# Sparse attention and a gated MLP on one Trainium2 core: the rows of q and k of heads 6 and 7 are loaded first, on both queues, and the first lines of the first batch's list of steps are set anew

## The chip, the cores and the metric

The kernel runs on one core of a Trainium2 chip as a single program. The metric is device time in microseconds (us) of one execution. The core has five engines that run their own instruction streams and meet at semaphores: PE (matmuls and transposes), DVE (vector work), ACT (activations, copies and, here, also DMA issues), POOL (vector work, memsets) and SP (DMA issues alone). DMAs are issued from two queues in this kernel, SP's and ACT's.

## What is computed

Attention over 8 batches and 8 heads of 576 tokens with 64 features each; heads 0 to 3 see a local window of 32 tokens, heads 4 to 7 see every 32nd token. Its output, heads side by side, is the input x of a gated MLP with a spatial gate (a 576 x 576 matrix over the tokens). Everything is float32.

```python
scores = np.matmul(q, k.transpose(0, 1, 3, 2)) / np.sqrt(D)
mask_local   = (rel >= 0) & (rel < 32)
mask_strided = (rel >= 0) & (pos[None, :] % 32 == pos[:, None] % 32)
scores = np.where(mask, scores, -1e9)          # heads 0-3 local, 4-7 strided
attn = np.exp(scores - scores.max(-1, keepdims=True))
attn = attn / (attn.sum(-1, keepdims=True) + 1e-9)
x = np.matmul(attn, v)                          # (8, 576, 512)
h = gelu_tanh(x @ w_in)
u, v = h[..., :512], h[..., 512:]
v_n = layernorm(v) * g_ln
v_s = np.einsum('ts,bsd->btd', w_sg, v_n) + b_sg[None, :, None]
out = x + (u * v_s) @ w_out
```

## The kernel before

The kernel treats the 8 batches one after the other. All its work is cut into some 80 kinds of steps, each a small function, and three hand-written lists set the order in which the steps are written out: `START` for the first batch (with everything that has to be loaded or converted once), `CYCLE` for the middle batches and `LAST` for the last one. A word of a list names a step, and after a colon which piece. `=` marks work that belongs to no batch, `-` work of this batch, no sign work for the next batch, `+` work for the one after it. A `^` sends those parts of a step that can go to either of two engines to the second one (loads from SP to ACT, some vector work between DVE and POOL). Each engine executes its instructions in the order in which the lists emit them, with no reordering by a scheduler, and the DMAs of both queues are numbered in the order of the lists too. Eight DMA semaphores are handed out in turn to that numbered sequence, so the ninth DMA waits, on the queue that issues it, until the first has landed, and so on: at most eight are under way, and a queue that waits for a slot holds back everything behind it.

The steps that matter here:

- **Rows of q and k** (`LP`, function `qk_rows`, line 449). For a pair of heads `hh` (0 and 1 are local, 2 and 3 strided; pair 3 is heads 6 and 7) four DMAs of 144 KB bring in two heads of q and two of k, by 96 partitions in pieces of 256 bytes. `TP` (`qk_turn`) transposes one of the two tiles on PE in six pieces; its argument is 2 x pair, plus 1 for k, so `TP:6` is q of pair 3 and `TP:7` its k. `TC` (`qk_turned`) copies the result from PSUM to `qT` or `kT` on ACT. The row tiles share four buffers.
- **Scores and softmax of pair 3**: `SS:3` (64 matmul instructions in the trace, tile `ss`), `MK:3` adds the mask on DVE (two instructions, tile `sms`), `MX:3` the maximum and `SB^:3` the subtraction on DVE, `EX:3` the exponential on ACT. `SL:0` and `SL:1` are the scores of the local pairs (tile `sa`), `MK:4` the mask of their first part (tile `sml`, `sm_mask`), on DVE.
- **Conversion of the weights.** `w_in` and `w_out` come as 64-bit floats and are turned into two float32 parts with integer operations. `w_in` has eight pieces of 512 KB (`cl:0` to `cl:7`, tile `stage`), `w_out` eight of 256 KB (`cl:8` and on, tile `cs`). A piece goes through `ca` (exponent field, DVE), `cb` (ACT), `cc` (two instructions, DVE), `cd` (ACT), `ce` (low word, DVE; with `^` on ACT and then POOL), `cf` (value, POOL; with `^` DVE), `cg` (high part, ACT) and `ch` (low part, POOL; with `^` DVE).
- **Later in the first batch**: `LP:2` loads the rows of pair 2, issued from ACT; `wb` and `wc` clear and load the bias row `bst`; `wl:1` loads a block of the token matrix (`wsg`). The matmuls of the MLP proper begin with `v` (tiles `v`, from `va:0` on).

Every instruction that goes through the recording helper shows line 83, so groups are told apart by their tiles.

Of the kernel before, what the change touches and what calls it, by code (L numbers as in the profile page):

```python
# [21 lines left out]


START = """
mk= mp= cl=:3 ca=:3 cl=:1 LP-^:3 cb=:3 cc=:3 ca=:1 cb=:1 cl=:0 cc=:1 cd=:1 cd=:3 cl=:2 TZ-:0
ca=:2 cl=:8 ml= ce=:3 ca=:0 cb=:0 ce=^:1 TP-^:6 TC-:6 cb=:2 TP-^:7 TC-:7 cf=^:1 cg=:1 cc=:2
cd=:2 LP-:0 SS-:3 LP-:1 TZ-:1 ca=:8 cb=:8 ch=:1 cc=:0 cd=:0 cl=:9 ce=^:0 TP-:1 MK-:3 TP-:0 TC-:0
MX-:3 SB-^:3 TC-:1 ce=:2 EX-:3 cf=^:2 LP-^:2 TP-^:2 TC-:2 SL-^:0 MK-:4 ca=:9 TP-^:3 TC-:3 SL-:1
MX-:4 wb= SB-:4 cl=:6 ca=:6 cb=:6 cc=:6 cl=^:4 cc=:8 LZ-:0 wc= wd= we= LZ-:1 wl=:1 MK-:5 MX-:5
cf=^:3 EX-:4 TP-:4 TC-:4 SU-:4 SB-:5 LP:1 SU-:3 cg=:2 ch=:2 cd=:8 TP-:5 cf=:0 wt=:1 TC-:5 SS-^:2  # L30
cd=:6 cg=:3 cl=^:7 EX-:5 mr= ML-:4 SU-:5 TP^:2 TC:2 MK-:2 MX-:2 cg=:0 ch=:0 TZ:0 ce=^:6 LV-:0
ML-^:5 ca=:4 TP:3 TZ:1 TC:3 wh=:1 ch=:3 wm=:1 ca=:7 SB-^:2 PL-:4 CL-:4 PL-^:5 CL-:5 CM-:5 VX-:0
VY-:0 XR-:0 EX-:2 SU-:2 cb=:4 cc=:4 ML-^:2 LP:0 TP^:0 cb=:7 LV-:1 TC:0 XHa-:0 XLa-:0 ce=^:8
cf=:8 TP^:1 TC:1 cb=:9 cc=:9 XHb-:0 XLb-:0 cf=^:6 cl=:5 PS-^:2 CS-:2 ca=:5 XD-:0 SL^:0 SL:1 MK:0
VA-:1 XH-:1 XL-:1 cd=:4 cc=:7 LV-:2 PV-^:2 PW-:2 XH-:2 cd=:9 ce=:9 wo= wp= ML-:3 LP:2 XR-:1 MX:0
PS-:3 CS-:3 cb=:5 SB:0 XD-:1 va:0 vb:0 cl=^:13 TP^:4 TC:4 XL-:2 vc:0 LV-:3 PV-:3 XR-:2 PW-:3
cd=:7 XH-:3 cc=:5 TP^:5 EX:0 ce=:4 cf=^:4 cg=:4 ch=:4 va:1 XL-:3 xt LP:3 vd:0 g:0 XD-:2 vb:1
ce=:7 XR-:3 cf=^:9 ls:0 lr^:0 wl=:0 TP^:6 TC:6 cd=:5 cl=^:15 vc:1 cf=:7 cg=:7 cg=:9 vd:1 TP:7
# [3 lines left out]
ca=:15 ca=:10 cb=:10 cb=:15 u:0 SU:0 wh=:4 cc=:10 wl=:3 wm=:4 cc=:15 cd=:10 ce=:10 cf=:10 MK:2  # L42
wt=:2 LQ+:0 ug:0 wh=:2 wm=:2 cl=^:11 wt=^:3 wh=:3 wm=:3 ML:0 lh:2 ll:2 cg=:13 u:3 ll:1 cd=:15
ca=:11 ce=^:15 cb=:11 cc=:11 PL:0 CL:0 ch=:13 ug:3 MX:3 SB^:3 s:3 cd=:11 ce=:11 cf=:11 cg=:11
CM:0 s^:2 cf=^:15 MX:2 SB^:2 s^:0 ch=^:11 sm:3 sm:2 cl=^:12 ca=:12 TZ+:1 EX:3 SU:3 sh:2 sl:2 s:1
sh:3 cb=:12 ML^:3 LZ:0 cg=:10 cc=:12 VA^:1 cd=:12 LQ+:3 sm:0 ch=:8 cg=:15 cl=:14 ch=^:10 ca=:14
ch=^:15 ce=^:12 cf=:12 sh:0 sl^:0 TQ+:0 cg=:12 LV:0 sm:1 sh:1 sl:1 r cb=:14 cc=:14 EX:2 LQ+:1
VA:0 XR:1 PS:3 CS:3 o:0 o^:1 ch=:12 sl:3 cd=:14 ce=:14 cf=^:14 cg=:14 SU:2 ML^:2 XH:0 XL:0
ch=:14 XH:1 XL:1 LV:3 o^:2 o^:3 o2:2 os:2 XD:1 XR:0 XD:0 o2:0 o2:3 os:3 LV:2 PS^:2 o2:1 PV:3
# [52 lines left out]
def tile_sparse_attention_moe(  # L102
# [14 lines left out]
    pe, dve, act, pool, sp = (  # L117
        InOrder(tc, e) for e in (nc.tensor, nc.vector, nc.scalar, nc.gpsimd, nc.sync)
    )
# [9 lines left out]
    TP = S // NCL  # L129
# [14 lines left out]
    def loads():  # L144

        return act if alt[0] else sp
# [299 lines left out]

        return b < 2

    def qk_rows(b, hh):

        for nm, src in (("q", q), ("k", k)):
            raw = p1.tile([P, RT, 2, D], F32, tag="raw", name=f"row{nm}_{b}_{hh}", bufs=4)
            for hp in range(2):
                loads().dma_start(
                    raw[0:RP, :, hp], src[b, 2 * hh + hp].rearrange("(p c) d -> p c d", c=RT)
                )
            state[b, hh, "row" + nm] = raw
# [506 lines left out]
    def out_send(b, kk):  # L964
# [6 lines left out]

    STEPS = {

        "LQ": qk_load, "LP": qk_rows, "TP": qk_turn, "TC": qk_turned, "TQ": qk_transpose, "LV": v_load, "TZ": k_zeros, "LZ": v_zeros, "SL": local_scores,
        "SS": strided_scores, "MK": sm_mask, "MX": sm_max, "SB": sm_sub, "EX": sm_exp,
        "SU": sm_sum, "ML": sm_mul, "PL": local_pt, "CL": local_pt_copy, "CM": local_pt_last,
        "VA": lambda b, hh: local_pv(b, hh, range(NJ)),
# [81 lines left out]
```

## Time and profile before

| | us |
|---|---|
| median of 3 runs | 581.92 |
| the three runs | 580.87, 581.92, 583.30 |
| span of the profiled execution, first to last instruction | 581.7 |
| PE busy | 550.2 (95% of the span) |
| DVE busy | 398.9 (69%) |
| ACT busy | 270.4 (46%) |
| POOL busy | 190.1 (33%) |

The page gives the span of the profiled execution and nothing around it; the median of the runs lies 0.2 us above that span, and their spread is 2.4 us. PE is busy almost throughout. Its idle time is found in the first tenth of the span, where weights are converted, the first heads are loaded and the first softmaxes run; that is the part that the change touches. To read it, take the views by stretch of time (how busy each engine is from here to there), the chain of waits (what released the work that ended last) and the timeline (each instruction with its start).

### The profile page before, as it was taken

Reading aid. Unit: us, or ns where it says so; the run is one execution under the profiler, and the core shown is the slowest. Engines: PE = TensorE matmul, PEld = TensorE weight load, DVE = VectorE, ACT = ScalarE, POOL = GpSimd, SP = SyncE. Lnnn points to the kernel's source line nnn. Section 1 sums busy time; section 2 is a strip of 40 time slices with the busy share of each in tenths; the row PEclk is TensorE's granted clock in tenths of the full one; section 3 lists DMA queues with packets and bytes.
Section 4 is the critical chain, followed back from the end, with each engine's and each line's share of the span. In section 5 each row is a group of like instructions: output and inputs, shape, how many; then the busy total and the mean of one; then the engine's idle time right before and its main releaser. Section 6 shows DMA issues by size and latency. Waiting matters only on the chain.

```text
span 581.7 us, 14975 instructions
## 1 busy us (share of the span) xinstructions
PE 550.2 (95%) x6129; PEld 493.7 (85%) x6129; DVE 398.9 (69%) x692; ACT 270.4 (46%) x396; POOL 190.1 (33%) x452
## 2 busy tenths in 40 slices
PE   0778999999899999999999999999999999999996
PEld 0667798978898889988998889988998889988995
DVE  4798898877774687567874687567774686545532
ACT  4566766622662248332652258332662247433320
POOL 3363484201722045311722045311722045302310
PEclk9986999999999999999999999999999999999999
DMA  8796665868832894259922894259822870055002
GB/s 233 207 174 161 141 159 92 188 138 151 186 55 61 177 192 72 42 134 176 171 42 65 175 195 67 41 137 177 167 42 61 180 177 1 1 122 155 2 1 90
DMA packets 261478, 69.95 MB, mean 120 GB/s; under 512 B 247137, under 2 KB 247137, under 8 KB 261410
## 3 DMA queue, kind: packets, MB, share of 16 engines
q1 hardware_dynamic: 172386, 46.11, 37.4%
q10 hardware_dynamic: 89024, 22.88, 18.6%
q8 instruction: 48, 0.79, 0.6%
q14 instruction: 20, 0.16, 0.1%
HBM read 50.09 MB, written 18.87 MB: 119 GB/s over the span
## 4 chain that ended last, share of the span: by engine, by line
PE 64%; DVE 11%; POOL 7%; ACT 5%; DMA 5%; issue 5%; ACTq 2%; SPq 0%; DVEq 0%; POOLq 0%
PE sg L83 18%; PE o L83 15%; PE v L83 11%; PE u L83 7%; POOL nt L83 4%; PE os L83 3%; PE ol L83 3%; ACTq L83 2%; POOL y L83 2%; PE pts L83 2%; DMA rowk<-in_k_dram 2%; PE sa L83 2%; DVE sr L83 1%; ACT L83 1%; ACT vg L83 1%
## 5 line engine op out<-in xcount | busy, mean ns | idle before, releaser
L83 PE MATMUL sg<-wsh,vg 128*128 128x288 f32 x512 | 113.2, 296 | 1.0 <-ACT ptl L83 0.8
L83 PE MATMUL u<-xt,wih 128*128 128x288 f32 x512 | 104.1, 298 | 2.6 <-ACT u L83 2.4
L83 PE MATMUL o<-woh,vg 128*128 128x512 f32 x288 | 95.5, 397 | 0.0
L83 PEld LDWEIGHTS sg<-wsh,vg 128*128 128x128 f32 x512 | 85.5, 188 | 2.0 <-ACT ptl L83 1.0
L83 PEld LDWEIGHTS u<-xt,wih 128*128 128x128 f32 x512 | 82.0, 188 | 4.8 <-ACT u L83 3.7
L83 PE MATMUL v<-wih,xt 128*128 128x512 f32 x256 | 83.9, 397 | 0.0
L83 ACT ACT_TABLE_LOAD x40 | 51.3, 1283 | 53.4 <-DMA xd<-xs 33.9
L83 PE MATMUL u<-xt,wil 128*128 128x288 f32 x256 | 75.5, 295 | 0.0
L83 PE MATMUL sg<-wsl,vg 128*128 128x288 f32 x256 | 75.3, 294 | 0.0
L83 PEld LDWEIGHTS o<-woh,vg 128*128 128x128 f32 x288 | 54.1, 188 | 11.1
L83 PEld LDWEIGHTS v<-wih,xt 128*128 128x128 f32 x256 | 48.0, 188 | 11.0
L83 PE MATMUL o<-wol,vg 128*128 128x512 f32 x144 | 56.3, 391 | 0.0
L83 DVE TENSOR_TENSOR ob<-o,xn 128x512 f32<-128x512 f32 x32 | 22.1, 689 | 44.4 <-PE o L83 43.6
L83 ACT CAST vg<-gt 128x576 fp32r<-128x576 f32 (+2 forms) x48 | 22.8, 509 | 61.1 <-DVE gt L83 61.1
L83 PE MATMUL v<-wil,xt 128*128 128x512 f32 x128 | 50.1, 392 | 0.0
L83 PEld LDWEIGHTS sg<-wsl,vg 128*128 128x128 f32 x256 | 48.2, 188 | 0.0
L83 PEld LDWEIGHTS u<-xt,wil 128*128 128x128 f32 x256 | 48.0, 188 | 0.1
L83 DVE TENSOR_TENSOR gt<-sg,u 128x576 f32<-128x576 f32 x32 | 23.6, 739 | 22.1 <-PE sg L83 12.4
L83 DVE BATCH_NORM_STATS2 bnst<-hv 128x6 f32<-128x512 f32 (+1 forms) x40 | 27.1, 676 | 16.8 <-ACT hv L83 16.8
L83 POOL TENSOR_TENSOR sms<-sms,sr 100x576 f32<-100x576 f32 x13 | 15.1, 1160 | 61.1 <-DVE sr L83 61.1
L83 DVE SCALAR_TENSOR_TENSOR vg<-hv,y,vg 128x512 fp32r<-128x512 f32 x32 | 23.0, 761 | 15.7 <-ACT vg L83 15.7
L83 PEld LDWEIGHTS o<-wol,vg 128*128 128x128 f32 x144 | 27.1, 188 | 4.9
(152 smaller groups left out, 1071.1 us busy)
## 6 DMA issues: line engine op xcount, KB each, us to landing
xd<-xs ACTq DMA_DIRECT2D x128, 72.0 KB
v<-in_v_dram SPq DMA_DIRECT2D x62, 144.0 KB
xn<-xd SPq DMA_DIRECT2D x8, 1024.0 KB
out_dram<-ob ACTq DMA_DIRECT2D x32, 256.0 KB
rawq<-in_q_dram SPq DMA_DIRECT2D x96, 72.0 KB
rawk<-in_k_dram SPq DMA_DIRECT2D x96, 72.0 KB
v<-in_v_dram SPq DMA_DIRECT2D x30, 128.0 KB
stage<-in_moe_w_in_dram SPq DMA_DIRECT2D x6, 512.0 KB
```

Source lines behind the costliest of these rows:

```text
L83: ins = self.tc.keep_in_program_order(op(*args, **kwargs))
```

## The change

Three things are edited. `qk_rows` takes a pair of queues and, where it is given one, issues q from the first and k from the second. A new step `LB` calls it with SP for q and ACT for k. And the first four lines of `START` are set anew: `LB-:3` stands at the very front in place of `LP-^:3` (which had all four DMAs on ACT, behind the first two pieces of `w_in` on SP), and the transposes, copies, scores and softmax of pair 3 and the loads of pair 0 and 1 stand earlier among the conversion steps.

```diff
 START = """
-mk= mp= cl=:3 ca=:3 cl=:1 LP-^:3 cb=:3 cc=:3 ca=:1 cb=:1 cl=:0 cc=:1 cd=:1 cd=:3 cl=:2 TZ-:0
-ca=:2 cl=:8 ml= ce=:3 ca=:0 cb=:0 ce=^:1 TP-^:6 TC-:6 cb=:2 TP-^:7 TC-:7 cf=^:1 cg=:1 cc=:2
...
+LB-:3 mk= mp= cl=:3 cl=:1 TZ-:0 TP-^:6 TC-:6 TP-^:7 TC-:7 ca=:3 cb=:3 LP-:0 cl=:0 SS-:3 cc=:3
+ca=:1 cb=:1 ml= cd=:3 MK-:3 MX-:3 cl=:2 SB-^:3 cc=:1 cd=:1 EX-:3 ce=:3 LP-:1 TZ-:1 ca=:0 cb=:0 ce=^:1
...
-    def qk_rows(b, hh):
+    def qk_rows(b, hh, queues=None):
 
-        for nm, src in (("q", q), ("k", k)):
+        for x, (nm, src) in enumerate((("q", q), ("k", k))):
+            queue = queues[x] if queues else loads()
             raw = p1.tile([P, RT, 2, D], F32, tag="raw", name=f"row{nm}_{b}_{hh}", bufs=4)
             for hp in range(2):
-                loads().dma_start(
+                queue.dma_start(
...
+        "LP": qk_rows, "LB": lambda b, hh: qk_rows(b, hh, (sp, act)),
```

What this does to SP's queue, at its beginning, with the semaphores that each issue waits for (DMAHW0 to DMAHW7 are the eight slots; `stage` is a piece of `w_in`, `rowq_3` the q rows of pair 3, `rowq_0` those of pair 0). Before:

```order
L83 DMA stage<-in_moe_w_in_dram 128x1024 x4
L83 DMA cs_147<-in_moe_w_out_dram 128x512 [waits DMAHW0_49]
L83 DMA rowq_0_204<-in_q_dram 96x6x64 [waits DMAHW1_49]
L83 DMA rowq_0_204<-in_q_dram 96x6x64 [waits DMAHW2_49]
L83 DMA rowk_0_207<-in_k_dram 96x6x64 [waits DMAHW3_49]
L83 DMA rowk_0_207<-in_k_dram 96x6x64 [waits DMAHW4_49]
```

and with the change, the same place:

```order
L83 DMA rowq_3_102<-in_q_dram 96x6x64 x2
L83 DMA stage<-in_moe_w_in_dram 128x1024 x2
L83 DMA rowq_0_152<-in_q_dram 96x6x64 x2
L83 DMA rowk_0_155<-in_k_dram 96x6x64 [waits DMAHW0_49]
L83 DMA rowk_0_155<-in_k_dram 96x6x64 [waits DMAHW1_49]
L83 DMA stage<-in_moe_w_in_dram 128x1024 [waits DMAHW2_49]
L83 DMA stage<-in_moe_w_in_dram 128x1024 [waits DMAHW3_49]
```

The q rows of pair 3 now go ahead of all weights, the rows of pair 0 ahead of the third and fourth piece, and these two pieces wait for slots 2 and 3, which the k rows of pair 3 (on ACT's queue) hold.

On ACT, from its first work to the DMAs of pair 2 (`cv` is a conversion buffer, `wih` the high part of `w_in`, `sms` the softmax tile of pair 3). Before:

```order
L83 DMA rowq_3_125<-in_q_dram 96x6x64 x2
L83 DMA rowk_3_128<-in_k_dram 96x6x64 x2
L83 ACTIVATE cv_122<-cv_122,ebias 128x512
L83 ACTIVATE cv_134<-cv_134,ebias 128x512
L83 ACTIVATE stage<-stage 128x512 x2
L83 ACTIVATE cv_175<-cv_175,ebias 128x512
L83 ACTIVATE stage<-stage 128x512
L83 COPY qT_3_187<-turnq_3_180 128x576
L83 ACTIVATE cv_145<-cv_145,ebias 128x512
L83 COPY kT_3_197<-turnk_3_190 128x576
```

and with the change:

```order
L83 DMA rowk_3_105<-in_k_dram 96x6x64 x2
L83 COPY qT_3_138<-turnq_3_131 128x576
L83 COPY kT_3_147<-turnk_3_140 128x576
L83 ACTIVATE cv_149<-cv_149,ebias 128x512
L83 ACTIVATE cv_194<-cv_194,ebias 128x512
L83 ACTIVATE stage<-stage 128x512 x2
L83 ACTIVATE sms_100<-sms_100 100x576
L83 ACTIVATE cv_242<-cv_242,ebias 128x512
L83 ACTIVATE stage<-stage 128x512
L83 COPY qT_0_263<-turnq_0_256 128x576
L83 COPY kT_0_129<-turnk_0_249 128x576
L83 ACTIVATE cv_266<-cv_266,ebias 128x512
```

Both copies of pair 3 now stand ahead of the first conversion step on ACT, and the exponential of pair 3 ahead of the third `cv`; behind these rows come, in both, the rest of the first conversions and then the DMAs of pair 2.

On DVE, from the second conversion on. Before:

```order
L83 SCALAR_TENSOR_TENSOR cv_134<-stage,cv_134 128x512
L83 TENSOR_SCALAR stage<-stage 128x512
L83 TENSOR_SCALAR cv_145<-stage 128x512
L83 SCALAR_TENSOR_TENSOR stage<-stage 128x512
L83 TENSOR_SCALAR cv_175<-stage 128x512
L83 TENSOR_TENSOR cv_134<-stage,cv_134 128x512
L83 SCALAR_TENSOR_TENSOR cv_145<-stage,cv_145 128x512
L83 TENSOR_SCALAR stage<-stage 128x512
L83 TENSOR_SCALAR cx<-cs_147 128x256
L83 SCALAR_TENSOR_TENSOR cv_175<-stage,cv_175 128x512
L83 TENSOR_SCALAR stage<-stage 128x512
L83 TENSOR_TENSOR sms_100<-ss_3_210,mask_s 36x576 x2
```

and with the change, from the same conversion buffer's first operation (`cv_194` is what `cv_134` was):

```order
L83 TENSOR_SCALAR cv_194<-stage 128x512
L83 TENSOR_TENSOR sms_100<-ss_3_159,mask_s 36x576 x2
L83 TENSOR_REDUCE mx_3_225<-sms_100 100x16
L83 TENSOR_TENSOR sms_100<-sms_100,mx_3_225 100x576
L83 SCALAR_TENSOR_TENSOR cv_194<-stage,cv_194 128x512
L83 TENSOR_SCALAR stage<-stage 128x512
L83 SCALAR_TENSOR_TENSOR stage<-stage 128x512
L83 TENSOR_SCALAR cv_242<-stage 128x512
L83 TENSOR_SCALAR cv_266<-stage 128x512
```

Mask, maximum and subtraction of pair 3 stood behind the first operations of all four pieces of `w_in` before; now they stand after those of the first piece and the exponent field of the second, and the rest of the conversions stands behind them. The number of instructions on each engine is the same, and the number of DMAs too; from the fifth line of `START` on the lists agree.

More of the change, by code (lines that the diff above doesn't have):

```diff
@@ L24 @@
 START = """
-mk= mp= cl=:3 ca=:3 cl=:1 LP-^:3 cb=:3 cc=:3 ca=:1 cb=:1 cl=:0 cc=:1 cd=:1 cd=:3 cl=:2 TZ-:0
-ca=:2 cl=:8 ml= ce=:3 ca=:0 cb=:0 ce=^:1 TP-^:6 TC-:6 cb=:2 TP-^:7 TC-:7 cf=^:1 cg=:1 cc=:2
-cd=:2 LP-:0 SS-:3 LP-:1 TZ-:1 ca=:8 cb=:8 ch=:1 cc=:0 cd=:0 cl=:9 ce=^:0 TP-:1 MK-:3 TP-:0 TC-:0
-MX-:3 SB-^:3 TC-:1 ce=:2 EX-:3 cf=^:2 LP-^:2 TP-^:2 TC-:2 SL-^:0 MK-:4 ca=:9 TP-^:3 TC-:3 SL-:1
+LB-:3 mk= mp= cl=:3 cl=:1 TZ-:0 TP-^:6 TC-:6 TP-^:7 TC-:7 ca=:3 cb=:3 LP-:0 cl=:0 SS-:3 cc=:3
+ca=:1 cb=:1 ml= cd=:3 MK-:3 MX-:3 cl=:2 SB-^:3 cc=:1 cd=:1 EX-:3 ce=:3 LP-:1 TZ-:1 ca=:0 cb=:0 ce=^:1
+cl=:8 TP-:1 TP-:0 TC-:0 TC-:1 ca=:2 cb=:2 cc=:0 cd=:0 cf=^:1 cg=:1 cc=:2 cd=:2 ch=:1 ca=:8 cb=:8
+cl=:9 ce=^:0 ce=:2 cf=^:2 LP-^:2 TP-^:2 TC-:2 SL-^:0 MK-:4 ca=:9 TP-^:3 TC-:3 SL-:1
 MX-:4 wb= SB-:4 cl=:6 ca=:6 cb=:6 cc=:6 cl=^:4 cc=:8 LZ-:0 wc= wd= we= LZ-:1 wl=:1 MK-:5 MX-:5
@@ L972, in tile_sparse_attention_moe @@
     STEPS = {
-        "LQ": qk_load, "LP": qk_rows, "TP": qk_turn, "TC": qk_turned, "TQ": qk_transpose, "LV": v_load, "TZ": k_zeros, "LZ": v_zeros, "SL": local_scores,
+        "LQ": qk_load, "LP": qk_rows, "LB": lambda b, hh: qk_rows(b, hh, (sp, act)),
+        "TP": qk_turn, "TC": qk_turned, "TQ": qk_transpose, "LV": v_load, "TZ": k_zeros, "LZ": v_zeros, "SL": local_scores,
         "SS": strided_scores, "MK": sm_mask, "MX": sm_max, "SB": sm_sub, "EX": sm_exp,
```

## The prediction

> **What bounds the kernel now.** I first read how busy each engine is by stretch (columns: from:to, length, busy time and instructions of PE, PE's weight loads, DVE, ACT, POOL, then the clock granted to PE, the DMA share, GB/s), because the change touches the opening alone.
>
> ```profile
> 0.00:5.00 5.00, 0.00 (x0) 0.00 (x0) 1.53 (x7) 1.49 (x2) 3.83 (x23) 1.00 0.49 173
> 5.00:28.00 23.00, 11.74 (x235) 10.38 (x238) 14.43 (x28) 12.80 (x21) 6.09 (x11) 1.00 0.90 227
> 28.00:48.00 20.00, 15.10 (x179) 12.76 (x168) 19.07 (x37) 14.57 (x29) 11.30 (x16) 0.78 0.91 185
> 56.00:576.00 520.00, 514.60 (x5503) 463.01 (x5502) 356.68 (x609) 237.97 (x340) 165.53 (x399) 1.00 0.54 112
> ```
>
> From 56 us on PE is busy 514.6 of 520 us: whatever makes that stretch start earlier or later moves the end by as much. From 28 to 48 DVE is busy 19.07 of 20 us and its order there is unchanged. Only from 5 to 28 us is there slack to win: DVE is busy 14.43 of 23 us. The chain of waits says what filled it:
>
> ```profile
> 3.70 10.45 DMA rowk<-in_k_dram
> 14.15 0.14 issue
> 14.29 1.21 PE turnk L83 x6
> 15.49 0.02 issue
> 15.52 0.65 ACT kT L83
> ...
> 27.39 0.70 DVE cv L83
> ...
> 47.16 1.55 PE pts L83 x8
> ...
> 55.92 2.79 PE v L83 x12
> ```
>
> The k rows of pair 3 (issued from ACT) landed at 14.15 us; from 27.39 on DVE's row of work sets the pace (first step `cc` of w_in piece 6), up to PE's matmuls. So the question is when DVE reaches that step, now 27.39 us. I call its shift **d**; the time is the old one plus d.
>
> **First part: when do the rows of pair 3 land (R)?** Now: 14.15.
>
> ```profile
> 0.79 1.95 SPq L83 DMA_DIRECT2D stage<-in_moe_w_in_dram  x4
> 1.07 1.41 ACTq L83 DMA_DIRECT2D rowq<-in_q_dram  x2
> 2.51 3.02 ACTq L83 DMA_DIRECT2D rowk<-in_k_dram  x2
> 5.24 0.49 DVE L83 TENSOR_SCALAR cv<-stage 128x512 int32<-128x512 int32 x1
> 1.00:2.00 1.00, 0.00 (x0) 0.00 (x0) 0.00 (x0) 1.00 (x1) 0.96 (x4) 1.00 0.04 8
> 4.00:10.00 6.00, 0.00 (x0) 0.00 (x0) 4.16 (x10) 1.46 (x3) 1.48 (x7) 1.00 1.04 343
> 15.00:19.00 4.00, 3.27 (x70) 2.91 (x70) 3.12 (x7) 3.32 (x6) 0.30 (x2) 1.00 0.93 207
> ```
>
> First bytes move at about 2.0 us (8 GB/s in the slice before it). While little but rows travel (15 to 19 us) the rate is 207 GB/s, with weights (4 to 10 us) 343. The four transfers of pair 3 are 4 x 147 KB = 590 KB, 2.85 us at 207. Landing costs a bit more: the first 524 KB piece needs 2.0 + 1.5 = 3.5 us at 343 GB/s and is read at 5.24, but DVE was busy until 5.2, so the lag is at most 1.7 us; I take half, 0.8. Early end: both queues share evenly from 2.0 us, R = 2.0 + 2.85 + 0.8 = 5.6. Late end of the likely case: ACT's transfers are served behind all that SP has queued at once, q rows and two pieces of w_in (1.05 MB, 3.05 us): R = 2.0 + 2.85 + 3.05 + 0.8 = 8.7. The row that speaks for late is the 10.45 us above, with four pieces of w_in ahead. **I take R = 7.0**, near the middle: no row has this mixture.
>
> The Trainium skill, "DMA: Bandwidth & Descriptors", section "Queues, rings and completion order", says that each DMA engine goes round the queues it has work for, a packet at a time. By that rule the even share and R = 5.6 would hold (580.0 by the sum below, the forecast's lower bound). The trace agrees only in part: ACT's rows, issued 0.3 us behind SP's first piece, had not all landed 13 us later.
>
> **Second part: from R to the mask on DVE.** PE starts 0.14 us behind the landing, the copy to `kT` 1.23 later, then scores and mask:
>
> ```profile
> 18.61 1.52 DVE L83 TENSOR_TENSOR sms<-ss,mask_s 36x576 f32<-36x576 f32 x2 [0.81 <-PE ss L83]
> 21.63 0.69 DVE L83 SCALAR_TENSOR_TENSOR stage<-stage 128x512 f32<-128x512 uint32 x1
> ```
>
> 14.15 to 18.61 is 4.46 us and none of it changes. So the mask starts at M = R + 4.46, at 11.5 instead of 18.6, and mask, maximum and subtraction hold DVE for 21.63 - 18.61 = 3.02 us. The two copies ahead of `cb:3` on ACT now make piece 3's first conversion wait for R as well (copy of k ends at R + 2.0, `cb` of 0.72 behind it, `cc` 1.15, `ca:1` 0.4: done at R + 4.3, just ahead of M), so it costs nothing beyond M.
>
> **Third part: what is late next.** Before, the conversions of all four pieces ran ahead of the mask, during the wait. Now those of pieces 1, 0 and 2 come behind it, and they go to and fro between DVE and ACT:
>
> ```profile
> 6.52 0.69 DVE L83 SCALAR_TENSOR_TENSOR cv<-stage,cv 128x512 int32<-128x512 int32 x1 [0.79 <-ACT cv L83]
> 7.24 0.43 DVE L83 TENSOR_SCALAR stage<-stage 128x512 int32<-128x512 int32 x1
> 8.04 0.72 ACT L83 ACTIVATE cv<-cv,ebias 128x512 int32<-128x512 int32 x1 [1.55 <-DVE cv L83]
> 9.98 1.20 ACT L83 ACTIVATE stage<-stage 128x512 f32<-128x512 int32 x2 [1.22 <-DVE stage L83]
> 13.70 1.04 POOL L83 TENSOR_TENSOR stage<-stage 128x512 f32<-128x512 f32 x1 [7.88 <-DMA rowq<-in_q_dram]
> 14.78 0.69 DVE L83 TENSOR_TENSOR cv<-stage,cv 128x512 f32<-128x512 f32 x1 [2.53 <-POOL stage L83]
> ```
>
> `cc` takes 0.72 + 0.43 = 1.15, an ACT operation 0.60 from start to start, `cb` 0.72 until another engine may go on. Counted from M: `cc:1` ends at 4.2; ACT: `cd:1` 4.2, `EX:3` 4.8, `cb:0` 5.4 to 6.1; DVE `cc:0` 6.1 to 7.3. ACT: `ce^:1` 6.0, two copies of pair 0 6.6, `cb:2` 7.7 to 8.5; POOL 6.7 to 7.7 and DVE `cf^:1` 7.7 to 8.4; `cc:2` 8.5 to 9.65. ACT: `cd:0` 8.4, `cg:1` 9.0, `cd:2` 9.7, `cb:8` 10.3, `ce^:0` 10.8; the DMAs of pair 2 start at M + 11.0. DVE's `ce:2` and `cf^:2` end at M + 11.8 and the local mask `MK:4` follows. Before, pair 2 was issued 3.3 us behind the mask. So of the 7.1 us by which M comes earlier, 7.7 are given back here. The issue itself is shorter then:
>
> ```profile
> 21.91 2.19 ACTq L83 DMA_DIRECT2D rowq<-in_q_dram  x2
> 24.13 1.32 ACTq L83 DMA_DIRECT2D rowk<-in_k_dram  x2
> 26.63 0.73 ACT L83 ACTIVATE cv<-cv,ebias 128x512 int32<-128x512 int32 x1
> 26.28 1.25 SPq L83 DMA_DIRECT2D rowq<-in_q_dram  x2
> ```
>
> It held ACT from 21.91 to 25.45, 3.54 us, waiting for slots; two such issues take 1.25 where none is taken, so four take 2.5, and the slots are free by then (rows of pairs 0 and 1 leave SP's queue by about 12 us). The two copies of pair 1 and the start of `cb:6` follow 1.18 us later, as from 25.45 to 26.63. `cb:6` starts at M + 11.0 + 2.5 + 1.18 = R + 19.1, against 26.63: **d = R - 7.5**. With R = 7.0, d = -0.5.
>
> **What is covered.** By bytes the third and fourth piece of w_in land at about 2.0 + 1.18 MB / 207 + 2.1 MB / 343 + 0.8 = 14.6 us, and are read at M + 5 = 16.5; without that cover each us late is one in d. Piece 6 of w_in may be loaded when `cf^:1` is done, M + 8.4 = 19.9, and needs at most 4.45 us as the first one (0.79 to 5.24), so 24.3; it is read behind `MK:4` at M + 13.3 = 24.8, cover 0.5 us. POOL clears `bst` behind its half of `ce^:0`, some 3 us later than before, and SP's load of `wsg` stands behind that, now at 25 us instead of 22.06:
>
> ```profile
> 31.57 1.27 PE L83 MATMUL wsgT<-ident,wsg 128*128 128x128 f32 x5
> 22.06 2.67 DMA wsg<-in_moe_w_sg_dram
> ```
>
> 25 + 2.67 = 27.7, needed at 31.57. From 27.39 on the order is the old one, and d goes through to the end.
>
> **Sum.** Span 581.7 - 0.5 = 581.2; the median of the runs stands 0.2 above the span, so **581.4 us**.
>
> **Rivals.**
>
> *ACT's rows come late and hold ACT (slower).* For: the only early transfers from ACT in the trace took until 12 to 14 us, and now both copies stand at the head of ACT's order, so every conversion waits for them; the third and fourth piece wait for their slots too. Against: only 0.3 MB of q rows and two pieces are ahead, not four. It decides from R = 7.5; at the old 10.45 us behind the end of issue (1.07 + 1.41) R = 12.9, d = +5.4, 587.3. Halfway between 8.7 and 12.9, R = 10.8: d = +3.3, **585.2**.
>
> *The clock of PE opens one step earlier.*
>
> ```profile
> 46.00:49.40 3.40, 3.20 (x56) 2.63 (x59) 2.99 (x7) 2.33 (x7) 2.61 (x4) 0.50 0.76 249
> 49.40:52.80 3.40, 3.40 (x130) 3.23 (x129) 2.54 (x5) 0.71 (x2) 2.07 (x3) 0.50 0.95 169
> 52.80:56.00 3.20, 2.83 (x62) 2.58 (x60) 2.19 (x5) 2.08 (x4) 0.00 (x0) 0.99 0.40 87
> 58.56 0.66 PE L83 MATMUL turnq<-ident,rowq 96*128 96x96 f32 x6
> ```
>
> PE runs at half clock from 49.4 to 52.8, though it was busy 3.20 of the 3.4 us before; six transposes take 0.66 us at full clock here and 1.21 in the chain at 14.29, where the clock column says 1.00, so that column can't be trusted at the start. If d = -0.5 fills the stretch before 49.4 enough for the clock to double there, at most half of 3.40 is saved, 1.7: 581.4 - 1.7 = **579.7**. Against: small matmuls and waits that a clock does not shorten fill much of it. The Trainium skill, "TensorE: Matmul & The Clock Gate", section "What's actually happening", has windows of 3.4 us that run freely and open the clock behind a busy one; the stretches at 0.50 fit that, and by it the step may fall either way from run to run.
>
> *The change does nothing to the end,* since DVE's row from 27.39 on is set by something else (piece 6, `bst`): **581.9**. For: covers of 0.5 us are thin.
>
> **Chances and range.** Forecast (R between 5.6 and 8.7, d -1.9 to +1.2, so 580.0 to 583.1): 0.63. Late rows: 0.17. Clock one step earlier: 0.10. No effect: 0.10. The range takes in the forecast's bounds, the clock's 579.7 with a little for an early R, and of the late rows the part up to d = +2.7: 579.5 to 584.6. About 0.5% (2.9 us) is what a measurement of this kernel can tell from no change. Faster than 579.0 needs the earlier clock and an early R together: 0.09. Slower than 584.8 needs R above 10.4, over half of the late rows, with a little from the thin covers: 0.13. Within: 0.78.
>
> **What would show it.** Right: `sms` masked on DVE near 11.5 us, the local mask `sml` near 23, ACT's issue of pair 2 near 22.5 and 2.5 us long, `cc` of piece 6 near 26.9, PE's `v` near 55.4. Wrong: ACT's first copy of pair 3 behind 9 us (late rows); a gap on DVE at piece 6; the clock's step from 0.50 in another place than 52.8; DVE's row from 27 to 47 us no longer closed, so that d is not passed on.

## The result, and the profile after

| | before | after |
|---|---|---|
| median of the runs, us | 581.43 (579.61 to 584.64, 18 runs) | 585.85 (582.53 to 588.46, 18 runs) |
| ratio to before | | 1.0069 (95% interval 1.0053 to 1.0085) |
| span of the profiled execution, us | 581.7 | 582.2 |

The kernel became slower by 0.7%, 4.0 us by the ratio. The forecast was 581.4 and its range ended at 584.6. The profiled execution after the change was one of the quicker ones, so that its span hides most of the loss; two further looks at the same kernel, below, are nearer to its median.

Busy time by stretch, after the change (columns as before):

```profile
0.00:5.00 5.00, 0.00 (x0) 0.00 (x0) 1.51 (x7) 1.49 (x2) 3.83 (x23) 1.00 0.56 122
5.00:28.00 23.00, 10.76 (x172) 9.10 (x172) 15.21 (x26) 10.94 (x19) 5.39 (x9) 1.00 0.88 206
28.00:48.00 20.00, 14.36 (x217) 12.02 (x218) 17.90 (x34) 14.44 (x27) 10.87 (x17) 0.81 1.10 202
56.00:576.00 520.00, 515.61 (x5517) 463.63 (x5514) 357.61 (x610) 239.28 (x342) 164.87 (x399) 1.00 0.54 113
```

Behind 56 us nothing differs: PE is busy 515.6 of 520 us. From 28 to 48 us DVE is no longer closed (17.90 of 20 us), because its row of work begins later (at 29.02 instead of 27.39 us) and stands still once more, for 0.50 us, at `wst`. The chain of waits of the same profile says where it is held:

```profile
1.81 7.10 DMA rowk<-in_k_dram
8.91 0.14 issue
9.05 1.21 PE turnk L83 x6
10.25 0.02 issue
10.28 0.65 ACT kT L83
...
13.35 0.75 DVE sms L83
...
24.45 0.57 ACTq L83
...
27.28 3.28 DMA bst<-in_moe_b_sg_dram
```

The chain still begins with the k rows of pair 3. They landed at 8.91 us, not at the forecast 7.0; that is 7.1 us after the second of the two transfers was issued. On DVE and ACT this reads as follows (start, duration, engine, operation, and in brackets the idle time before it and what ended it):

```profile
10.28 0.64 ACT L83 COPY kT<-turnk 128x576 f32<-128x576 f32 x1 [2.83 <-PE turnk L83]
11.57 0.69 DVE L83 SCALAR_TENSOR_TENSOR cv<-stage,cv 128x512 int32<-128x512 int32 x1 [2.84 <-ACT cv L83]
13.35 1.52 DVE L83 TENSOR_TENSOR sms<-ss,mask_s 36x576 f32<-36x576 f32 x2 [0.29 <-PE ss L83]
24.45 0.57 ACTq L83 DMA_DIRECT2D rowq<-in_q_dram  x1
25.83 1.26 ACTq L83 DMA_DIRECT2D rowk<-in_k_dram  x2
25.72 0.69 DVE L83 TENSOR_TENSOR sml<-sa,mask_l 128x512 f32<-128x512 f32 x1
29.02 0.69 DVE L83 SCALAR_TENSOR_TENSOR cv<-stage,cv 128x512 int32<-128x512 int32 x1 [1.35 <-ACT cv L83]
31.34 0.75 DVE L83 TENSOR_TENSOR wst<-bst,wst 1x576 fp32r<-1x576 f32 x1 [0.50 <-ACT wst L83]
```

The mask runs 5.3 us earlier than before (13.35 against 18.61), and yet the local mask `sml` is 2.2 us later (25.72 against 23.55) and `cc` of piece 6 is 1.63 us later (29.02 against 27.39). The copy of k and the conversion behind it stood still for 2.8 us each.

### The profile page after: what moved, and what is told of

It is laid out like the page before. It is cut to its first block, busy times and chain, and to the rows that moved or that the text cites. A ratio compares the mean times of both kernels' runs of the same rounds, so it can differ in the third digit from the quotient of the medians.

```text
span 582.2 us, 14974 instructions
## 1 busy us (share of the span) xinstructions
PE 550.1 (94%) x6129; PEld 492.8 (85%) x6129; DVE 399.7 (69%) x692; ACT 270.0 (46%) x396; POOL 189.7 (33%) x452
## 4 chain that ended last, share of the span: by engine, by line
PE 71%; DVE 11%; POOL 4%; ACT 4%; issue 4%; DMA 4%; ACTq 2%; SPq 0%; DVEq 0%; POOLq 0%
PE sg L83 18%; PE o L83 15%; PE v L83 14%; PE u L83 11%; PE os L83 3%; PE ol L83 3%; POOL nt L83 2%; PE sa L83 2%; PE pts L83 2%; ACTq L83 2%; PE ss L83 2%; DVE sr L83 1%; DVE sms L83 1%; DMA rowk<-in_k_dram 1%; POOL y L83 1%
## 5 line engine op out<-in xcount | busy, mean ns | idle before, releaser
L83 PEld LDWEIGHTS o<-woh,vg 128*128 128x128 f32 x288 | 54.1, 188 | 11.1
L83 DVE TENSOR_TENSOR gt<-sg,u 128x576 f32<-128x576 f32 x32 | 23.6, 739 | 22.1 <-PE sg L83 12.4
L83 PEld LDWEIGHTS o<-wol,vg 128*128 128x128 f32 x144 | 27.1, 188 | 4.9
```

The costliest lines, as they stand in the source:

```text
L83: ins = self.tc.keep_in_program_order(op(*args, **kwargs))
```

## The experiments

Theory **A**: the half of the rows that goes through ACT's queue lands late beside the weights on SP's, and d follows R. Rival **B**: the new order loses by itself, whenever the rows land. Rival **C**: the loss arises behind 56 us, by PE's clock. All but `as_is_2` were timed against the kernel before.

### The changed kernel twice more, and the kernel before once more

No edit.

> The changed kernel once more, for a second trace. Theory A (the k rows of pair 3, on ACT's queue, land late at about 9 us and hold ACT and DVE): k rows used by PE at 9 us again, cc of w_in piece 6 on DVE at about 29.0, the matmul row 2.1 us behind, and a ratio near 1.007. Rival C (the loss lies in PE's clock steps or elsewhere behind 56 us, and the opening only carries 1 to 2 us of it): the shift seen on DVE at 40 us is again 2 us, but grows behind 56 us to the 4 us that the medians show.

> The changed kernel, a third look at where its k rows land. Theory A: R between 8.5 and 12, typically near 11.3 as in three of the four profiles so far in which a half of the first rows went through ACT's queue beside w_in; cc of piece 6 at R + 19.9 (27.39 + R - 7.5), within 0.4 us. If cc of piece 6 does not follow R, the formula fell.

> The kernel before, once more, as a control: its ratio to itself says what a difference of nothing looks like, and its profile shows how far one execution of it differs from another. Ratio 0.998 to 1.002; k rows of pair 3 landed at 14.15 in the first profile; by theory A they land at 13.5 to 14.8 again, since four pieces of w_in or w_out are ahead of them in both, and DVE's steps up to 50 us lie within 0.5 us of the first profile. If R of the kernel before moves by 2 us or more and its time does not, then d = R - 7.5 has the wrong reference.

The changed kernel again: 585.46 us, ratio 1.0074 (1.0047 to 1.0101); the third look is a single execution, without a ratio. The kernel before against itself: 1.0 (0.9985 to 1.0015), so about 0.15% is what nothing looks like. PE's first transposes of k, and DVE's `cc` of piece 6, in the timelines of `as_is`, `as_is_2` and `before_again`, in this order:

```profile
11.80 1.19 PE L83 MATMUL turnk<-ident,rowk 96*128 96x96 f32 x6 [4.53 <-DMA rowk<-in_k_dram]
31.65 0.69 DVE L83 SCALAR_TENSOR_TENSOR cv<-stage,cv 128x512 int32<-128x512 int32 x1 [1.35 <-ACT cv L83]
```

```profile
11.02 1.19 PE L83 MATMUL turnk<-ident,rowk 96*128 96x96 f32 x6 [3.74 <-DMA rowk<-in_k_dram]
30.91 0.69 DVE L83 SCALAR_TENSOR_TENSOR cv<-stage,cv 128x512 int32<-128x512 int32 x1 [1.35 <-ACT cv L83]
```

```profile
14.02 1.19 PE L83 MATMUL turnk<-ident,rowk 96*128 96x96 f32 x6 [1.23 <-DMA rowk<-in_k_dram]
26.96 0.69 DVE L83 SCALAR_TENSOR_TENSOR cv<-stage,cv 128x512 int32<-128x512 int32 x1 [1.76 <-ACT cv L83]
```

The loss is there again, as A has it, and by 32 us already. From PE's first `v` (56.82, 59.18 and 60.04 us in the three looks at the change, 55.70 and 54.58 before) to the end of the span it is 525.4, 527.2 and 525.2 us with the change and 526.0 and 525.0 before. The means are 0.4 us apart, a tenth of the loss, so C falls. Taking off the 0.14 us between landing and first transpose, R was 11.66 and 10.88 in the two further looks, so the 8.91 of the first profile was an early one, and the 9 us and 29.0 us that were expected of `as_is` were missed by some 2.7 us each. In `as_is_2` `cc` of piece 6 came at R + 20.03, where R + 19.9 was expected. R of the kernel before is steady (14.15 and 13.88), and its `cc` of piece 6 came 0.4 us apart. The changed kernel's R moves by 2.8 us from run to run, and `cc` of piece 6 with it.

### One queue in place of two

```diff
-        "LB": lambda b, hh: qk_rows(b, hh, (sp, act)),
+        "LB": lambda b, hh: qk_rows(b, hh, (sp, sp)),
```

> Only the queue of the four first transfers is changed: k of pair 3 follows q on SP, ahead of the weights. Theory A: all four land by about 6.8 us, the mask of pair 3 starts near 11.3, cc of piece 6 near 26.9 (shift -0.7 plus up to 0.5 for bst), ratio 0.997 to 1.001. Rival B (the new order of steps loses by itself, conversions behind the mask go to and fro between DVE and ACT, whenever the rows land): ratio 1.004 or more, cc of piece 6 behind 28.5 though the rows are early.

581.91 us, ratio 1.0025 (1.0003 to 1.0046). This one edit took away most of the loss; the unedited change, timed beside it, had 1.0074. PE, DVE's first conversion and DVE's `cc` of piece 6 in its timeline:

```profile
7.12 1.20 PE L83 MATMUL turnk<-ident,rowk 96*128 96x96 f32 x6 [0.97 <-DMA rowk<-in_k_dram]
9.04 0.43 DVE L83 TENSOR_SCALAR cv<-stage 128x512 int32<-128x512 int32 x1 [3.83 <-DMA stage<-in_moe_w_in_dram]
11.66 1.51 DVE L83 TENSOR_TENSOR sms<-ss,mask_s 36x576 f32<-36x576 f32 x2
27.46 0.69 DVE L83 SCALAR_TENSOR_TENSOR cv<-stage,cv 128x512 int32<-128x512 int32 x1 [1.51 <-ACT cv L83]
```

R is 6.98, just the 7.0 that was forecast, and the mask is at 11.66 (forecast 11.5). Even so `cc` of piece 6 is not earlier than before, 27.46 against 27.39. The ratio lies above A's upper end (1.001) and below B's lower one (1.004), though its interval reaches both; `cc` of piece 6 is well ahead of B's 28.5. So late rows are most of the loss, but the rest of A, a small gain at R = 7.0, did not come. The 0.25% that is left in the time is not seen in this one profile, whose span is 579.7 us (581.7 and 579.6 before); where it arises was not found. DVE did not wait for the rows here: it waited 3.83 us for the first piece of `w_in`, which it read at 9.04 (5.24 before).

### The two queues exchanged

```diff
-        "LB": lambda b, hh: qk_rows(b, hh, (sp, act)),
+        "LB": lambda b, hh: qk_rows(b, hh, (act, sp)),
```

> The changed kernel with the two queues of the first rows exchanged: q of pair 3 from ACT, k from SP. Theory A (the rows that go through ACT's queue land late beside w_in on SP's, whichever tensor they are): now the q rows land at 8 to 12 us, turnq starts then (5.6 in the changed kernel) and turnk right behind it, both copies on ACT wait as long, and the time is 1.005 to 1.010 of that before. Rival T (it lies with the k tensor or with the last transfers of the four): turnq still before 7 us, turnk still at 9 to 12.

586.46 us, ratio 1.009 (1.0071 to 1.011). PE's timeline:

```profile
11.39 1.19 PE L83 MATMUL turnq<-ident,rowq 96*128 96x96 f32 x6 [11.39 <-DMA rowk<-in_k_dram]
12.38 1.17 PE L83 MATMUL turnk<-ident,rowk 96*128 96x96 f32 x6
```

Now the q rows are the late ones. (The row names `rowk` as what ended the wait; the instruction that waits reads q alone, whose transfer was the last to land.) It is the queue, not the tensor, and rival T falls.

### Rows of pair 0 between the first rows and the weights

```diff
-LB-:3 mk= mp= cl=:3 cl=:1 TZ-:0 ... ca=:3 cb=:3 LP-:0 cl=:0 SS-:3 cc=:3
+LB-:3 mk= mp= LP-:0 cl=:3 cl=:1 TZ-:0 ... ca=:3 cb=:3 cl=:0 SS-:3 cc=:3
```

> The changed kernel, but the four transfers of pair 0's rows stand ahead of the first two pieces of w_in on SP's queue; the k rows of pair 3 stay on ACT's queue. R is the landing of the last k rows, seen as the first transpose turnk on PE. Theory P (the two queues take turns a packet at a time; a packet of w_in is 4 KB and one of a row 256 bytes, so beside weights the rows get few bytes, and beside other rows they get half): R at 5.6 to 7.3, because the k rows have rows beside them and the weights come behind. Theory S (ACT's queue is served behind what SP has queued, whatever its packets): 1.18 MB of rows at 207 GB/s go first, R at 8.5 or later, as in the changed kernel (8.9). By both the first piece of w_in lands later (2.0 + 5.7 + 1.5 + 0.8 = 10.0 us; 8.3 in the changed kernel), so that DVE's first conversion and not R sets the mask, at about 12.7, and the time is 1.002 to 1.006 of that before. What decides is R, not the time.

583.86 us, ratio 1.0039 (1.0023 to 1.0056). The k rows go through ACT's queue as in the changed kernel, but what lies beside them on SP's queue is rows. The view by DMA queue counts packets, MB and the share of time in a stretch; q1 is SP's queue, q10 ACT's. A packet of `w_in` is 4 KB in the trace (a piece of 512 KB in 128 packets), one of a row 256 bytes. First the kernel before from 7 to 8.5 us, where SP's queue moves weights alone and ACT's the rows of pair 3:

```profile
q1 hardware_dynamic: 128, 0.46, 89.3%
q10 hardware_dynamic: 121, 0.03, 9.6%
```

Then the changed kernel in `as_is` from 5.5 to 7 us:

```profile
q1 hardware_dynamic: 96, 0.36, 94.0%
q10 hardware_dynamic: 75, 0.02, 5.6%
```

Then `rows_first`, from 4 to 5.5 us and from 5.5 to 7 us:

```profile
q1 hardware_dynamic: 725, 0.18, 68.3%
q10 hardware_dynamic: 548, 0.14, 47.5%
```

```profile
q1 hardware_dynamic: 1203, 0.30, 134.1%
q10 hardware_dynamic: 31, 0.01, 2.9%
```

Beside rows the two queues moved 725 and 548 packets, 0.18 and 0.14 MB: not far from an even share, and ACT's part was done before 7 us (from 7 to 9 us the view shows no q10 at all). Beside weights the kernel before moved 128 and 121 packets (139 and 145 in `before_again`), an even share by packets, and yet 0.46 against 0.03 MB. The turns are not exact: in the half us before this stretch the counts were 38 and 10, in the us behind it 110 and 167. The stretch of the changed kernel shows the same small share of the bytes (0.02 MB against 0.36), but its counts say less, since most of ACT's rows had been moved by then (1027 of its 1184 packets, from 2 to 5.5 us). The trace keeps sixteen landing marks (increments of its semaphore) for every transfer, the last of which is its landing. For the last transfer of the k rows they stand at, in us:

| kernel | first ten marks | last six marks |
|---|---|---|
| one queue | 5.57 to 5.90 | 5.91, 5.95, 6.11, 6.12, 6.78, 6.98 |
| rows of pair 0 first | 5.65 to 6.06 | 6.20, 6.45, 6.56, 6.59, 6.69, 6.77 |
| the change, first profile | 5.50 to 7.67 | 7.73, 7.75, 7.80, 7.81, 8.17, 8.91 |
| the change, `as_is_2` | 5.77 to 7.67 | 8.65, 9.17, 9.27, 9.35, 10.58, 10.88 |
| the change, `as_is` | 5.71 to 6.28 | 7.48, 7.90, 8.67, 10.51, 10.55, 11.66 |

So with weights beside them the rows are not late as a whole. In `as_is` ten of sixteen parts landed almost as early as on one queue, and a few stragglers made the 11.66. In this run and in `as_is_2` the last of them came within 0.3 us of the last mark of SP's second piece of `w_in` (11.42 and 10.72); in the first profile it came well before it (8.91 against 10.51). By the marks R is 6.77 in `rows_first`, as theory P had it (5.6 to 7.3), and not 8.5 or later: S falls. That P's turns make the stragglers too fits the counts, but why some parts are early and others late in one transfer was not found. No gain in time was to be had, as both theories had said: the first weights land late now, and they set the mask (13.32; 12.7 was expected).

```profile
7.59 1.17 PE L83 MATMUL turnk<-ident,rowk 96*128 96x96 f32 x6
10.70 0.43 DVE L83 TENSOR_SCALAR cv<-stage 128x512 int32<-128x512 int32 x1 [5.70 <-DMA stage<-in_moe_w_in_dram]
13.32 1.52 DVE L83 TENSOR_TENSOR sms<-ss,mask_s 36x576 f32<-36x576 f32 x2
28.96 0.69 DVE L83 SCALAR_TENSOR_TENSOR cv<-stage,cv 128x512 int32<-128x512 int32 x1 [1.34 <-ACT cv L83]
```

The mask stands at 13.32, as in the first profile of the change (13.35), for another reason, and `cc` of piece 6 at 28.96 (29.02 there). What counts is when the mask runs, whatever makes it so.

### Each half of the change alone

The transfers at the front, with the order of before for the rest:

```diff
+LB-:3 mk= mp= cl=:3 ca=:3 cl=:1 cb=:3 cc=:3 ca=:1 cb=:1 cl=:0 cc=:1 cd=:1 cd=:3 cl=:2 TZ-:0
...
```

> Loads first on both queues as in the change, but the steps in the order of before. Theory A: the rows land by 9 but the weights 3 us later than before, and DVE's mask of pair 3 stands behind the conversions as before, so cc of piece 6 comes about 2 us later than before, ratio 1.003 to 1.006. Rival B: without the new order nothing is lost, ratio 0.998 to 1.001.

The new order, with the rows behind the first two pieces of w_in, all from ACT, as before:

```diff
-LB-:3 mk= mp= cl=:3 cl=:1 TZ-:0 ...
+mk= mp= cl=:3 cl=:1 LP-^:3 TZ-:0 ...
```

> The new order of steps, with the rows of pair 3 all on ACT behind two pieces of w_in as before. Theory A: rows land at 12 to 13 instead of 8.9, d = R - 7.5 gives +4.5 to +5.5 at cc of piece 6, ratio 1.009 to 1.012. Rival B: about the same as the change, ratio 1.006 to 1.008.

The transfers alone: 583.46 us, 1.0053 (1.0037 to 1.0068). The order alone: 587.22 us, 1.0115 (1.0094 to 1.0136). Both ratios are where A put them, and neither half is good by itself. The steps behind them were met less well: the rows landed at 9.83 in the first (by 9 expected) and at 11.18 in the second (12 to 13 expected), and `cc` of piece 6 moved by 1.35 and 3.90 us (about 2, and 4.5 to 5.5 expected). PE and DVE of the transfers alone:

```profile
9.97 1.19 PE L83 MATMUL turnk<-ident,rowk 96*128 96x96 f32 x6 [2.93 <-DMA rowk<-in_k_dram]
9.70 0.69 DVE L83 SCALAR_TENSOR_TENSOR cv<-stage,cv 128x512 int32<-128x512 int32 x1 [0.79 <-ACT cv L83]
20.88 1.52 DVE L83 TENSOR_TENSOR sms<-ss,mask_s 36x576 f32<-36x576 f32 x2
28.74 0.69 DVE L83 SCALAR_TENSOR_TENSOR cv<-stage,cv 128x512 int32<-128x512 int32 x1 [1.43 <-ACT cv L83]
```

Here DVE does not wait for rows any more, PE alone does (2.93 us). The weights behind them are late: the first `cc` runs at 9.70, 6.52 before, and DVE cannot make it up, so that it reaches piece 6 1.35 us late. In the order alone the rows wait for the weights: `turnk` starts at 11.32, the first `cc` at 13.85 and `cc` of piece 6 at 31.29.

### Copies behind the conversions

```diff
-... TP-^:7 TC-:7 ca=:3 cb=:3 LP-:0 cl=:0 SS-:3 cc=:3 ca=:1 cb=:1 ml= cd=:3 MK-:3 MX-:3 cl=:2 SB-^:3 cc=:1
+... TP-^:7 ca=:3 cb=:3 LP-:0 cl=:0 cc=:3 ca=:1 cb=:1 ml= cd=:3 cc=:1 TC-:7 SS-:3 MK-:3 MX-:3 cl=:2 SB-^:3
```

> The changed kernel, but ACT's copy of k of pair 3 and the scores stand behind the conversions of the first two pieces of w_in (cb and cc of both), so that a late landing of the k rows does not hold them up. Theory A (late rows cost by moving the mask, M = R + 4.46, and by the conversions that then stand behind the mask): with R at 11.3 the second step of the second piece (1.15 us on DVE) runs while the rows are waited for, but the copy may start later by some 0.5 us; local mask sml 0.5 to 0.8 us earlier than the 28.0 of bst_early at the same R, time 1.004 to 1.008 of that before. Rival (what is lost is lost because ACT stands still behind the copies): then all of the conversions come free, sml at 26 or earlier at R = 11.3 and the time at 1.002 or less.

585.39 us, ratio 1.0081 (1.0062 to 1.0101). PE and DVE:

```profile
10.50 1.19 PE L83 MATMUL turnk<-ident,rowk 96*128 96x96 f32 x6 [3.49 <-DMA rowk<-in_k_dram]
12.07 0.69 DVE L83 SCALAR_TENSOR_TENSOR cv<-stage,cv 128x512 int32<-128x512 int32 x1 [0.79 <-ACT cv L83]
15.47 1.52 DVE L83 TENSOR_TENSOR sms<-ss,mask_s 36x576 f32<-36x576 f32 x2 [2.25 <-PE ss L83]
26.54 0.69 DVE L83 TENSOR_TENSOR sml<-sa,mask_l 128x512 f32<-128x512 f32 x1
```

R was 10.36 here. From the mask to `sml` it takes 11.07 us, against 12.3 to 12.4 in the changed kernel, so the 1.15 us of the second piece's step did come out of the row; but the mask starts 0.65 us later behind R (5.11 against 4.46), so some 0.5 us is left, as A said (at this R the changed kernel's `sml` would be near 27.1). The ratio lies just past A's upper end (1.008). The rival, that all of the loss is ACT standing still behind its copies, falls (it had the time at 1.002 or less): DVE now waits 2.25 us at the mask in place of the conversion.

### The bias row cleared early

```diff
-ca=:1 cb=:1 ml= cd=:3 ...
+ca=:1 cb=:1 ml= wb= cd=:3 ...
-MX-:4 wb= SB-:4 ...
+MX-:4 SB-:4 ...
```

> The changed kernel, but the step that clears the bias row bst stands two lines of the list earlier, so that POOL clears it before its share of the conversions and SP can load it earlier. Theory A (bst's late load added 0.4 to 0.5 us behind DVE's step cc of w_in piece 6, on top of what the late rows cost): from that cc to wst on DVE 1.85 us as before the change, against 2.32 in the changed kernel; R and everything up to that cc as in the changed kernel (R 8 to 12 us from run to run); time 1.004 to 1.008 of that before. Rival: bst is covered and the 0.47 us is something else; then cc to wst stays at 2.3 us.

586.34 us, ratio 1.0085 (1.0061 to 1.0108). PE, and DVE from `cc` of piece 6 to `wst`:

```profile
11.40 1.19 PE L83 MATMUL turnk<-ident,rowk 96*128 96x96 f32 x6 [4.37 <-DMA rowk<-in_k_dram]
31.27 0.69 DVE L83 SCALAR_TENSOR_TENSOR cv<-stage,cv 128x512 int32<-128x512 int32 x1 [1.35 <-ACT cv L83]
33.11 0.75 DVE L83 TENSOR_TENSOR wst<-bst,wst 1x576 fp32r<-1x576 f32 x1
```

The second step runs 1.84 us behind the first, which is A's number. But it proves nothing, for the unedited change has 1.85 us, here in `as_is`, where `cc` was at 31.65:

```profile
33.50 0.75 DVE L83 TENSOR_TENSOR wst<-bst,wst 1x576 fp32r<-1x576 f32 x1
```

The 0.5 us at `bst` in the first profile belongs to that execution, and was no term of the loss. What made that transfer take 3.28 us there was not tried.

### An attempt to beat both

```diff
-LB-:3 mk= mp= cl=:3 cl=:1 TZ-:0 TP-^:6 TC-:6 TP-^:7 TC-:7 ca=:3 cb=:3 LP-:0 cl=:0 SS-:3 cc=:3
-ca=:1 cb=:1 ml= cd=:3 MK-:3 MX-:3 cl=:2 SB-^:3 cc=:1 cd=:1 EX-:3 ce=:3 LP-:1 ...
+cl=:3 LB-:3 mk= mp= cl=:1 ca=:3 cb=:3 cc=:3 TZ-:0 TP-^:6 TC-:6 TP-^:7 TC-:7 ca=:1 cb=:1 cc=:1 LP-:0 cl=:0 SS-:3
+ml= cd=:3 MK-:3 MX-:3 cl=:2 SB-^:3 cd=:1 EX-:3 ce=:3 wb= LP-:1 ...
```

The diff leaves out that all four transfers go through SP's queue, as in the one-queue kernel, and that `wb=` goes from its old place, as with the bias row cleared early.

> One piece of w_in first on SP's queue, then the four transfers of pair 3 on SP's queue too, then the second piece; the second step of the conversion of the second piece stands ahead of the mask on DVE instead of behind it; bst is cleared early. Theory A (the rows must come through one queue, and putting rows ahead of all weights left DVE idle for 3.8 us until the first piece landed, which then had to be made up behind the mask): DVE starts the first conversion near 5.2 us as before the change, k rows land at 7 to 8.5, mask at 11.7 to 12.7, local mask sml at 22.4 to 23.2 (23.55 before), cc of piece 6 near 26.5 (27.39 before); time 0.997 to 1.000 of that before. Rival B (the new order of the steps loses by itself, whenever the rows land): sml behind 23.6 and the time at 1.003 or more.

582.34 us, ratio 1.002 (1.0004 to 1.0035): not faster than before. A missed, and rows, mask, `sml` and `cc` all came later than it had them; B's condition on `sml` is met, and its 1.003 lies inside the interval, so that this run doesn't decide against B. R was 8.62, the mask at 12.99, `sml` at 24.07, `cc` of piece 6 at 27.51. The saved 1.15 us is there (11.08 us from mask to `sml`), but the piece in front costs the rows 1.6 us against the one-queue kernel. No order that was run is faster than the kernel before; that none exists was not shown.

## Why the prediction was wrong

The step that failed is the first one, the moment R at which the rows land. Below are the steps of the prediction against all profiles in which the order from the mask on is that of the change (R is `turnk`'s start less 0.14; for the exchanged queues that of `turnq`; M is the mask on DVE):

| kernel | R | M | `cc` of piece 6 | from M to it |
|---|---|---|---|---|
| one queue | 6.98 | 11.66 | 27.46 | 15.80 |
| rows of pair 0 first | (7.45) | 13.32 | 28.96 | 15.64 |
| the change, first profile | 8.91 | 13.35 | 29.02 | 15.67 |
| the change, `as_is_2` | 10.88 | 15.25 | 30.91 | 15.66 |
| order alone | 11.18 | 15.65 | 31.29 | 15.64 |
| `bst` early | 11.26 | 15.62 | 31.27 | 15.65 |
| the change, `as_is` | 11.66 | 16.02 | 31.65 | 15.63 |
| queues exchanged | 11.25 | 16.57 | 32.22 | 15.65 |

In brackets: there `turnk` came right behind `turnq`, and the k rows had landed earlier (at 6.77 by the marks).

- **First part, R: this is the step that failed.** It took 7.0, the middle between an even share of the two queues (5.6) and ACT's rows served behind all of SP's (8.7). The changed kernel had 8.91, 11.66 and 10.88, beyond even the late end. Both ends were wrong. The early one read an even share as equal bytes, and took all parts of a transfer to land together: beside 4 KB packets the rows' 256 bytes go slowly, and the few parts that are held up set R. The late one let two pieces of `w_in` land by 8.7 us at 343 GB/s; the last mark of the second piece came at 10.51, 11.42 and 10.72, and from 5.5 to 7 us the rate was 222 GB/s in the first profile and 253 in `as_is`. That ACT's queue beside SP's weights is what makes R late is shown by the exchanged queues, the one queue and the rows of pair 0 in between. The profile of the kernel before already had the row that was needed, 128 packets against 121 and 0.46 MB against 0.03; the prediction looked at bytes of both queues together. The rule cited from the Trainium skill, "DMA: Bandwidth & Descriptors", section "Queues, rings and completion order", speaks of turns at whole packets, and these counts agree with it, with one difference: it puts some 9 to 17 descriptors into a packet, and the even counts here are of single pieces of 256 bytes and of 4 KB. What was wrong was the 5.6 us worked out from it. The remark against the late case, that only 0.3 MB and two pieces were ahead, didn't ask how long these two take beside other transfers.
- **Second part, M = R + 4.46: right where rows are late, with a term left out.** It was 4.44 us in the first profile, 4.36 and 4.37 in the others of the change. Piece 3's conversion was done just ahead of the mask, as worked out: DVE was idle for 0.29 us between them. Left out was the first piece of `w_in`, which now stands behind rows on SP's queue: DVE read it at 8.31, 9.36 and 8.99 us with the change, 5.24 before. Where the weights and not the rows set the mask, it runs 2.62 us behind that read (9.04 to 11.66 on one queue, 10.70 to 13.32 with the rows of pair 0 first). So in the first profile the mask could not have run before 10.9, and d = -0.8 was the most to be had there (10.9 + 15.65 against 27.39); the forecast's lower bound, d = -1.9, was out of reach however early the rows came.
- **Third part, what is late next: right, a quarter of a microsecond short.** Pair 2 was to be issued at M + 11.0; it was at 24.45, M + 11.1. The issue was to take 2.5 us and took 2.64 (24.45 to 27.09). `cc` of piece 6 stands at M + 15.63 to M + 15.80 in every kernel of this order, against 15.4 by the prediction's row (M + 14.64 for `cb:6`, and 0.76 to `cc`). With this the formula becomes d = R - 7.3 in place of R - 7.5. So the point from which the change loses, M = 27.39 - 15.65 = 11.74, is just where the mask comes when the rows land at 7.0 to 7.3 us: at the R that was forecast, DVE reaches piece 6 no earlier than before, as the one-queue kernel's 27.46 shows. The reference itself is known to 0.4 us (27.39 and 26.96).
- **What is covered:** piece 6 was there in time; `bst` was late by 0.5 us in one of three looks.
- **Sum:** the three looks at the change have a mean R of 10.5, for which the corrected formula gives d = 3.2; the two later ones alone, 11.3, give 4.0. The ratio's 1.0069 is 4.0 us of 581.43. In the profiles, as means of the three looks and of the two before, `cc` of piece 6 is 3.4 us later, PE's first `v` 3.5 and the span's end 3.9 (584.6 against 580.7). So most of the loss is made before piece 6, and d goes through to the end on average. In a single execution it can differ: that of `as_is` took 7.4 us more than the median of the kernel before in its session, with `cc` of piece 6 4.3 us late, while in `copy_behind` the two agree (2.4 and 2.5). The ratios of the edited kernels, too, stand for 0.4 to 2.8 us more than `cc` of piece 6 moved in their one profile (order alone: 6.7 against 3.9). What adds this was not found.
- **Rivals:** "ACT's rows come late and hold ACT" is what happened: in the first profile ACT stood still for 2.83 us ahead of the copy of k. Its price, 585.2 at R = 10.8, is near the measured 585.85, and its chance of 0.17 was too small, by the same error. That 10.8 was the middle between two bounds, so that its nearness to the looks is in part luck. "The clock opens one step earlier" didn't happen: PE's stretch at half clock ended at 54.2 us in the first profile, later than the 52.8 of before (the rows below). Whether the clock's steps are what makes the stretch from PE's first `v` to the end differ between executions (525.0 to 527.2 us) was not tried. "Nothing" is nearly what the one-queue version does.

```profile
50.80:54.20 3.40, 3.40 (x152) 3.23 (x154) 2.57 (x5) 1.36 (x2) 2.71 (x4) 0.50 0.91 160
54.20:57.60 3.40, 3.40 (x77) 3.19 (x74) 2.68 (x7) 2.30 (x5) 0.00 (x0) 1.00 0.65 150
```

- **B**, that the order loses by itself, is a small part at most where the rows are early: with R at 7.0 DVE reaches piece 6 as before, and what the time still loses is 0.25% (0.03 to 0.46%). That the order can't win, because the conversions behind the mask then set DVE's pace, fits both one-queue versions and is not shown beyond them.

## What to carry to other kernels

Before a transfer of small pieces is moved to a second queue, look at what runs beside it on the other queue: here the two queues shared by packets rather than by bytes, and the last of the small packets beside large ones came late, at a moment that varied from run to run. Putting an urgent load behind the others on one queue can land earlier than giving it a queue of its own (6.98 us against 8.9 to 11.7 here). And a load brought forward pushes another one back: work out the point at which the gain is nothing (here a mask at 11.74 us) before asking how likely the forecast moment is.

## What was unexpected of the hardware

The same second half of the k rows, 147 KB, issued from ACT's queue at 1.8 us, was complete by 7 us with rows beside it, but took until 8.9, 10.9 and 11.7 us in three executions of one kernel with weights beside it. It was not late as a whole: in the latest of the three, ten of its sixteen parts had landed by 6.3 us. What decides which parts straggle, and so the moment within that range, was not found.
